# Fused attention and two feed-forward layers on one core: last block's bias rows doubled by DMA, first weight units split on ScalarE and VectorE, four small items moved within a step

## The chip, the cores and the metric

The kernel runs on one core of a Trainium2 chip. The metric is the device time of one execution in microseconds (us). The time before is the median of three executions. The profile is of one more execution of the same program.

## The reference

Attention with a learned relative-position bias, then two feed-forward layers, all in float32. B = 2, H = 8, S = 576, D = 64; 1152 tokens, model width 512, hidden width 2048.

```python
scores = (q @ k^T) / sqrt(D)                            # B, H, S, S
x = log1p(abs(i - j)) / log1p(max(i, 1))                # S, S
bias = relu(x * w1 + b1) @ w2                           # 32 hidden, then H
attn = softmax(scores + bias)
x = (attn @ v) as 1152 tokens x 512
h = x @ w_in;  x = (relu(h) + alpha * min(h, 0)) @ w_out
h = x @ w_in2; x = (P(h) / (Q(h) + 1e-6)) @ w_out2      # P cubic, Q quadratic in abs(h)
```

## The kernel before

**Blocks and steps.** The query rows are cut into nine blocks: four groups of 128 rows for each of the two batches, and a last block 8 that holds the remaining 64 rows of both batches. A block takes four steps, one for each pair of heads, so there are 36 steps, n = 0 to 35. In step n TensorE computes the scores of that step (L326) into PSUM, VectorE adds the bias and takes the row maximum (`row_max`, L338, once for each head of the pair: u = 0 and 1), ScalarE takes the exponential and its row sums (`expo`, L349), TensorE transposes the result (`flip` u = 0, 1 and 2, L365 and L361), ScalarE or VectorE copies the transposes out of PSUM (`flip_out`, L377 on ScalarE, L371 and L375 on VectorE), and TensorE multiplies with the values (L389). The steps overlap: the transposes of step n run in step n + 1 and its values in step n + 2. The scores have two PSUM buffers, one for each u; so the scores of step n + 1 wait for both row maxima of step n, and for `flip_out` 2, which reads a spare corner of the second buffer. After step 35 the same banks hold the first hidden tiles of the feed-forward part.

**Bias rows.** Beside the steps the bias of the next group of rows is made, one eighth in each step: `hidden` (L228 on ScalarE, L230 on VectorE), a matmul in two halves (`bias_mm`, L244, into a PSUM tile with a single buffer, so each half waits until the one before it has been copied out), the copies `bias_out` (L256 on ScalarE, L258 on VectorE) and a DMA that brings the rows into place (`bias_move`, L270). The last block has four such parts; two DMAs of 64 rows for each (L274) fill partitions 0 to 63 of the bias tile, for one batch, and `bias_again` (L278) copies them to partitions 64 to 127, two heads at a time, on VectorE, in steps 29 to 32.

**End of a block.** `inverse` (L400 to L402) inverts the row sums. For blocks 0 to 5 the inverse goes through a transpose (`inverse_flip`, L407) and DRAM to all partitions; from block 6 on `inverse_on_tensor` (L434) spreads it with 16 matmuls. `block_out` (L423) copies the values' result out of PSUM, `block_scale` (L442) multiplies it with the inverse on VectorE, and `block_split` cuts it into a high part (L450, ScalarE) and a low part (L451, GpSimd).

**Weights.** The weights come in units of 128 x 512, 64 in all. For each, `unit_load` (L603 or L605) loads it as pairs of words, `unit_rest` and `unit_scale` (L617, L613) work on ScalarE, `unit_join` (L621, L624) on VectorE; then `unit_high` rounds to the high part and `unit_low` subtracts it. For units 0 to 11 the high part is made on VectorE (L646) and the low part on GpSimd (L651); for the others on ScalarE (L644) and VectorE (L651). Units 0 to 4 are made during steps 30 to 35.

**Feed-forward part.** `up` (L682) and `down` (L697) matmuls run in pairs from step 35 on, each product as three matmuls of high and low parts.

**What sets the order.** The order of the instructions on each engine is written out by hand: each item gets a due time in an agenda, `ag.at(time, function, ...)`, and all items are issued in the order of these times. The times come from a table `Z` and from `step_time(n)`; they are no waits. Each engine runs its own instructions in this order and waits only for data and for buffers. So a change of a due time changes the place of an instruction in its engine's queue, and nothing else.

Of the kernel before, what the change touches and what calls it, by code (L numbers as in the profile page):

```python
# [11 lines left out]
F32 = mybir.dt.float32  # L12
# [4 lines left out]
ALU = mybir.AluOpType  # L17
# [3 lines left out]
B, H, S, D = 2, 8, 576, 64  # L21
# [29 lines left out]
def row_tables():  # L51
# [35 lines left out]
    
}
# [17 lines left out]
def fused_kernel(ctx: ExitStack, tc: tile.TileContext, qT, q4T, kT, vp, m1_in, m1_out, m2_in, m2_out, small, ttab, out):  # L106
    nc = tc.nc
# [9 lines left out]
    ag = Agenda()  # L117
# [96 lines left out]
    bias, hid, bev, bps = {}, {}, {}, {}  # L214
# [52 lines left out]
    def bias_move(j, r):  # L267
        be, bt = bev.pop((j, r)), bias[j]
        if j < 4:
            nc.sync.dma_start(out=bt[r::8].rearrange("p h j -> p (h j)"), in_=be)  # L270
        else:
            for i in range(2):
                rows = bt[2 * r + i : 64 : 8].rearrange("p h j -> p (h j)")
                nc.sync.dma_start(out=rows, in_=be[64 * i : 64 * i + 64])  # L274

    def bias_again(h):

        nc.vector.tensor_copy(out=bias[4][64:, h : h + 2], in_=bias[4][:64, h : h + 2])  # L278

    def bias_rows_beside(j, r, at, step, at0, step0):  # L280

        z, z0 = step / 4.1, step0 / 4.1
        for c in range(4):
            ag.at(at0 + z0 * Z[f"hidden{c}"], hidden, j, r, c)
        for u in range(2):
            x = at + Z[f"bias_mm{u}"] * z
            n = max((n for n in range(FIRST, LAST) if step_time(n) <= x), default=None)
            if n is None:
                ag.at(x, bias_mm, j, r, u)
                t = at + Z[f"bias_out{u}"] * z  # L290
            else:
                t = max(x, step_time(n) + Z["beside"])
                ag.at(t, bias_mm, j, r, u)
                key = "scalar" if f"bias_scalar_{j}{u}" in ON else "vector"
                t = max(step_time(n) + Z[f"bo_{key}{int(t - step_time(n) >= Z['values'])}"], t + 0.1)
            ag.at(t, bias_out, j, r, u)
        ag.at(max(at + Z["bias_move"] * z, t + 0.1), bias_move, j, r)

    def bias_rows(j, r, at, step, at0, step0):
        z, z0 = step / 4.1, step0 / 4.1  # L300
        for c in range(4):
            ag.at(at0 + z0 * Z[f"hidden{c}"], hidden, j, r, c)
        ag.at(at + Z["bias_mm0"] * z, bias_mm, j, r, 0)
        ag.at(at + Z["bias_out0"] * z, bias_out, j, r, 0)
        ag.at(at + Z["bias_mm1"] * z, bias_mm, j, r, 1)
        ag.at(at + (1.6 * step if j == 0 else Z["bias_out1"] * z), bias_out, j, r, 1)
        ag.at(at + Z["bias_move"] * z, bias_move, j, r)


    FIRST, LAST = 8, 36  # L310
# [115 lines left out]
    def by_tensor(k):  # L426
        return k >= 6
# [25 lines left out]
    DT, DT2, DT3 = 4.1, Z["dt2"], Z["dt3"]  # L453
# [16 lines left out]
    def step_time(n):  # L470
        t = T0
        for a, b, dt in ((0, 4, DT0), (4, 24, DT), (24, 32, DT2), (32, 99, DT3)):
            t += max(0, min(n, b) - a) * dt
        return t

    rows = [(0, r, Z["row0"] + r * Z["row_step"], Z["row_step"]) for r in range(8)]
# [11 lines left out]
    for n in range(NSTEP):  # L488
        t = step_time(n)
        k, hp = divmod(n, 4)  # L490
        next_t, new = step_time(n + 1), FIRST <= n + 1 < LAST
        ag.at(t, scores, n)
        for u in range(2):
            ag.at(t + Z["max0"] + Z["max1"] * u, row_max, n, u)
            ag.at(t + Z["expo0"] + Z["expo1"] * u, expo, n, u)
            ag.at(next_t + Z[f"new_flip{u}"] if new else t + DT + Z["flip0"] + Z["flip1"] * u, flip, n, u)
            ag.at(t + DT + Z["fout0"] + Z["fout1"] * u, flip_out, n, u)
        ag.at(next_t + Z["new_flip2"] if new else t + DT + Z["flip2"], flip, n, 2)
        ag.at(next_t + Z["new_fout2"] if new else t + DT + Z["fout2"], flip_out, n, 2)
        ag.at(t + 2 * DT + Z["values"], values, n)  # L500
        if hp == 3:
            ag.at(t + Z["inv"], inverse, k)
            scale = t + 3 * DT + Z["new_bscale"] if FIRST <= n + 2 < LAST else t + 3 * DT + Z["bscale"]
            if by_tensor(k):
                ag.at(scale - 0.1, inverse_on_tensor, k)
            else:
                at = step_time(n + 2) - 0.06 if FIRST <= n + 2 else t + DT + Z["iflip"]
                ag.at(at, inverse_flip, k)
                ag.at(at + 1.2, inverse_spread, k)
            ag.at(t + 3 * DT + Z["bout"], block_out, k)  # L510
            ag.at(scale, block_scale, k)
            ag.at(scale + Z["bsplit"] - Z["bscale"], block_split, k)
        if hp == 0 and k + 1 < len(BLOCKS):
            ag.at(t + Z["loadq"], load_q, k + 1)
# [5 lines left out]
    TAIL, TB = 3, Z["tb"]  # L520
    GB, NB, NT2 = 3, 3, 2
    NWA, NWC, NWB, NMID, NSP = 5, 2, 13, 13, 3
    UHS, USP = 12, 48
    NW = NWA + NWC + NWB
    t35 = step_time(NSTEP - 1)
    M0 = t35 + Z["m0"]
# [13 lines left out]
    now, p, d = M1, TAIL, 0  # L540
# [22 lines left out]
    wt, raws, mids, away = {}, {}, {}, {}  # L563
# [74 lines left out]
    def unit_high(j):  # L638
        slot = j % NW
        pool = pools["wa" if slot < NWA else "wc" if slot < NWA + NWC else "wb"][1]  # L640
        wt[units[j]] = pool.tile([P, 2, 512], F32R, tag="w", name="w")
        out = wt[units[j]][:, 0, :]
        if j >= UHS:
            nc.scalar.copy(out=out, in_=mids[j])  # L644
        else:
            nc.vector.tensor_copy(out=out, in_=mids[j])  # L646

    def unit_low(j):
        w = wt[units[j]]
        eng = nc.gpsimd if j < UHS else nc.vector  # L650
        eng.tensor_tensor(out=w[:, 1, :], in0=mids.pop(j), in1=w[:, 0, :].bitcast(F32), op=ALU.subtract)  # L651

    def early(j, key):
        return Z[key + "_early" * (j < NWA)]
# [7 lines left out]
    def unit_two(j, t):  # L662
        ag.at(t, unit_high, j)
        ag.at(t + early(j, "ulow"), unit_low, j)
# [126 lines left out]
        nc.vector.memset(one, 1.0 + 1e-6)  # L791

    ag.at(step_time(20), moe_consts)
    for h in range(0, H, 2):
        ag.at(step_time(29 + h // 2) + Z["again"], bias_again, h)
    ag.at(EARLY, early_pools)
    ag.at(M0 - 0.1, psum_u)
    ag.at(M1 - 0.1, late_psum)
# [9 lines left out]
    for p in range(NPAIR):  # L808
        ly, g, c, f = blocks[2 * p]
        t = u_t[2 * p + 1]  # L810
# [20 lines left out]
    for k in range(NU):  # L831
        ly, g, c, f = blocks[k]
        if f == groups[ly][g][-1]:
            for m in range(4 - ly):
                t = max(0.01 + 0.01 * m, HB * (m + 1) / (4 - ly) + Z[f"dadd{ly}"]) + d_t[k]
# [8 lines left out]
    for j in range(len(units)):  # L844
        t = one_t[-1] + Z["ud0" if j < 16 else "ud" if j < 22 else "ud2x"] if j else EARLY + Z["u0"]
        if j < NWA:
            t = max(t, two_t[j - 2] + early(j, "ulow") + 0.1 if j > 1 else 0.0)
        else:
            t = max(t, NEXT + 0.1 if j < NWA + NMID else two_t[j - NMID] + Z["ulow"] + 0.1 if j < USP else 0.0)
        one_t.append(t)  # L850
        t += early(j, "utwo")
        if j:
            t = max(t, two_t[-1] + early(j, "ud2"))
        if j >= NWA:
            t = max(t, NEXT + 0.1 if j < NWA + NWC else LATE + 0.2 if j < NW else released[j - NW] + 0.1)
# [67 lines left out]
```

## Time and profile before

| | |
|---|---|
| median of 3 executions | 604.25 us (603.94 to 604.37) |
| the profiled execution | 604.18 us |
| its span, first to last instruction | 602.4 us |
| around the span | 1.8 us |
| mean granted TensorE clock | 0.997 |
| busy: TensorE matmul / weight load | 586.9 / 504.3 us |
| busy: VectorE / ScalarE / GpSimd | 500.1 / 427.4 / 41.7 us |

In the profile PE is TensorE, PEld its weight load, DVE VectorE, ACT ScalarE, POOL GpSimd, and SP the engine that issues DMAs. Busy shares are averages over stages with different limits. Matmuls are pipelined, so a TensorE that shows as busy may still be waiting within a group; the distance from the scores of one step to those of the next shows more than the busy share does.

### The profile page before, as it was taken

To read this page: it belongs to the slowest core of one execution; us is meant where nothing else is said; L and a number is where in the kernel's file an instruction comes from. 1 tells how busy PE (TensorE), PEld (TensorE's weight loads), DVE (VectorE), ACT (ScalarE), POOL (GpSimd) and SP (SyncE) were. 2 spreads that over 40 slices of the span, in tenths; PEclk is the share of its full clock that TensorE was granted. 3 is DMA by queue.
4 is the path that set the end of the run, shared out by engine and by line. 5 is a ranking of instruction groups with operands and counts; after the bars stand their busy time and mean duration, and the time that the engine had idled before them with its cause. 6 is when DMAs were issued, how large, how long until landed. Compare 5 with 4: busy or idle time off the path is not lost.

```text
span 602.4 us, 11747 instructions
## 1 busy us (share of the span) xinstructions
PE 586.9 (97%) x4678; PEld 504.3 (84%) x4678; DVE 500.1 (83%) x837; ACT 427.4 (71%) x716; POOL 41.7 (7%) x35
## 2 busy tenths in 40 slices
PE   8899999999989999999999999999999999999997
PEld 5356666666767999999999999998999999899985
DVE  6687788887698967779998779989999999779783
ACT  6678889888777656576675567797777887655660
POOL 0000000000022321000000302100000000000000
PEclk9899999999999999999999999999999999999999
DMA  5893323342723334344555477767000000001011
GB/s 169 263 231 107 92 73 103 81 104 62 187 72 100 112 106 139 114 154 156 172 149 174 131 207 217 215 203 262 19 2 1 0 1 0 2 2 52 1 52 54
DMA packets 41239, 65.31 MB, mean 108 GB/s; under 512 B 4016, under 2 KB 23776, under 8 KB 41184
## 3 DMA queue, kind: packets, MB, share of 16 engines
q1 hardware_dynamic: 41040, 64.21, 36.4%
q8 instruction: 37, 0.61, 0.4%
q10 hardware_dynamic: 144, 0.35, 0.2%
q14 instruction: 18, 0.15, 0.1%
HBM read 47.35 MB, written 6.58 MB: 90 GB/s over the span
## 4 chain that ended last, share of the span: by engine, by line
PE 83%; DVE 8%; ACT 4%; DMA 2%; issue 2%; SPq 0%; ACTq 0%; DVEq 0%
PE ops L697 30%; PE hps L682 30%; PE bps L244 6%; PE s L326 5%; PE pv L389 5%; PE tp L365 4%; DVE p L338 1%; DVE mid L621 1%; PE s L361 1%; ACT pt L377 1%; DVE mid L624 1%; DMA away<-mid 1%; DVE w L651 1%; ACT p L349 1%; DMA bias<-be 1%
## 5 line engine op out<-in xcount | busy, mean ns | idle before, releaser
L682 PE MATMUL hps<-xh,w 128*128 128x384 f32 x768 | 204.1, 336 | 0.0
L682 PEld LDWEIGHTS hps<-xh,w 128*128 128x128 f32 x768 | 139.6, 188 | 1.3 <-issue 0.2
L682 PE MATMUL hps<-xl,w 128*128 128x384 f32 x384 | 128.7, 335 | 0.0
L697 PE MATMUL ops<-g,w 128*128 128x384 f32 x576 | 104.5, 336 | 0.0
L697 PE MATMUL ops<-w,g 128*128 128x512 f32 x432 | 102.5, 392 | 1.2 <-DVE acc L769 1.2
L697 PEld LDWEIGHTS ops<-g,w 128*128 128x128 f32 x576 | 100.8, 188 | 0.0
L697 PEld LDWEIGHTS ops<-w,g 128*128 128x128 f32 x432 | 80.7, 188 | 17.6 <-issue 1.5
L349 ACT ACTIVATE p<-p,nm 128x576 f32<-128x576 f32 x72 | 55.7, 773 | 28.1 <-DVE nm L338 28.0
L682 PEld LDWEIGHTS hps<-xl,w 128*128 128x128 f32 x384 | 72.1, 188 | 0.9
L752 ACT CAST g<-n 128x768 fp32r<-128x768 f32 x48 | 40.1, 835 | 40.0 <-DVE n L716 28.3
L338 DVE CUSTOM_DVE_ANT_0 p<-s,bias 128x576 f32<-128x576 f32 x72 | 52.1, 753 | 14.1 <-PE s L326 8.9
L621 DVE SCALAR_TENSOR_TENSOR mid<-mid,raw 128x512 int32<-128x512 int32 x64 | 50.4, 787 | 12.5 <-ACT mid L613 12.4
L244 PE MATMUL bps<-h,w2s 128*32 128x288 f32 x576 | 51.4, 421 | 5.0 <-DVE be L258 2.5
L230 DVE TENSOR_SCALAR h<-tt,sc,nb 128x576 f32<-128x576 f32 x98 | 53.4, 582 | 0.0
L757 DVE TENSOR_TENSOR g<-n,g 128x768 fp32r<-128x768 f32 x48 | 46.5, 968 | 7.8 <-ACT g L752 7.8
L624 DVE SCALAR_TENSOR_TENSOR mid<-raw,mid 128x512 int32<-128x512 int32 x64 | 50.3, 786 | 2.2
L326 PE MATMUL s<-kt,q 64*128 64x288 f32 (+1 forms) x320 | 46.1, 433 | 1.4 <-DVE nm L338 0.8
L389 PE MATMUL pv<-pt,v 128*32 128x128 f32 (+2 forms) x1200 | 46.8, 267 | 0.0
L389 PEld LDWEIGHTS pv<-pt,v 128*32 128x32 f32 (+1 forms) x1200 | 40.4, 119 | 7.3 <-issue 2.7
L617 ACT ACTIVATE raw<-raw 128x512 int32<-128x512 uint32 x64 | 43.4, 678 | 2.7 <-DMA raw<-in_moe_w_in_dram 1.4
L613 ACT ACTIVATE mid<-raw 128x512 f32<-128x512 f32 x64 | 42.4, 662 | 0.0
L228 ACT ACTIVATE h<-tt,sm,sc 128x576 f32<-128x576 f32 x46 | 39.3, 863 | 3.0 <-DVE sc L172 2.5
(75 smaller groups left out, 734.4 us busy)
## 6 DMA issues: line engine op xcount, KB each, us to landing
raw<-in_moe_w_in_dram SPq DMA_DIRECT2D x32, 512.0 KB, 4.6
raw<-in_moe_w_out_dram SPq DMA_DIRECT2D x32, 512.0 KB, 3.7
bias<-be SPq DMA_DIRECT2D x32, 288.0 KB, 4.1
away<-mid SPq DMA_DIRECT2D x16, 256.0 KB, 4.9
mid<-away SPq DMA_DIRECT2D x16, 256.0 KB, 4.2
v<-in_vp_dram SPq DMA_DIRECT2D x10, 256.0 KB, 6.8
kt<-in_kT_dram SPq DMA_DIRECT2D x8, 288.0 KB, 5.7
out_dram<-acc SPq DMA_DIRECT2D x9, 256.0 KB, 2.1
```

The costliest lines, as they stand in the source:

```text
L230: nc.vector.tensor_scalar(out=h, in0=x, scalar1=sc[:, k : k + 1], scalar2=nb1, op0=ALU.mult, op1=ALU.max)
L244: nc.tensor.matmul(out=ps[32 * c : 32 * c + 32], lhsT=w2s, rhs=hid[j, r, c][:, u * HALF : (u + 1) * HALF], start=True, stop=True,)
L326: nc.tensor.matmul(out=pps[n, u][cols, w, :HALF], lhsT=queries[k][rows, hp, cols], rhs=KT[bb][rows, hp, w * HALF : (w + 1) * HALF], start= ...
L338: nc.vector.tensor_tensor_reduce(out=ptile[n][:, u, :].rearrange("p (w j) -> p w j", w=2), in0=pps.pop((n, u))[:, :, :HALF], in1=bias[j][: ...
L349: nc.scalar.activation(out=p, in_=p, func=AF.Exp, bias=nms.pop((n, u)), scale=-1.0, accum_out=sums[k][:, h : h + 1])
L389: nc.tensor.matmul(out=pv[64 * u + d : 64 * u + d + wide, hp, cols], lhsT=V[bb][:, j, 2 * hp + u, d : d + wide], rhs=pt[:, 4 * u + j if j ...
L617: nc.scalar.activation(out=low, in_=low.bitcast(U32), func=AF.Copy, scale=0.90625 * 2.0 ** -29, bias=0.24)
L621: nc.vector.scalar_tensor_tensor(out=m, in0=m, scalar=3, in1=raw[:, :, 0], op0=ALU.logical_shift_left, op1=ALU.bitwise_or)
L624: nc.vector.scalar_tensor_tensor(out=m, in0=raw[:, :, 1], scalar=-(2 ** 31), in1=m, op0=ALU.bitwise_and, op1=ALU.bitwise_or)
L682: nc.tensor.matmul(out=ps, lhsT=a, rhs=b, start=(i == 0), stop=(i == len(prs) - 1))
L697: nc.tensor.matmul(out=ops[ly, c, m], lhsT=a, rhs=b, start=(f == fs[0] and i == 0), stop=(f == fs[-1] and i == 2))
L757: nc.vector.tensor_tensor(out=gt[:, 1], in0=tmp.pop(p), in1=gt[:, 0].bitcast(F32), op=ALU.subtract)
```

## The change

1. `bias_move` for the last block issues four DMAs of 64 rows for each of the four parts instead of two: each half of `be` goes to partitions 0 to 63 and again to 64 to 127. `bias_again` and its four calls are gone.
2. For units 0 to 11 `unit_high` now runs on ScalarE and `unit_low` on VectorE, as for the other units.
3. `bo_scalar0` goes from 2.9 to 2.35: the `bias_out` on ScalarE is issued earlier in its step. In the queue this passes it ahead of another instruction at two places: ahead of a `hidden` in step 24, and ahead of a `block_split` in step 27.
4. `inverse` of blocks 1 to 7 moves from 4.03 to 5.65 after the start of the block's last step (`new_inv`): from ahead of the next step's `row_max` to behind it and behind `flip_out` 2.
5. `block_scale` of blocks 1 to 5 moves from 3.3 to 5.8 (`new_bscale`), and `block_split` with it: `block_scale` from the end of one step to behind the next step's row maxima, the high part of `block_split` from ahead of that step's two `expo` to behind them. Blocks 6 and 7 keep 3.3 (`new_iscale`).

The lines of the table `Z` that hold these numbers are left out of the diff.

```diff
         else:
-            for i in range(2):
-                rows = bt[2 * r + i : 64 : 8].rearrange("p h j -> p (h j)")
-                nc.sync.dma_start(out=rows, in_=be[64 * i : 64 * i + 64])
-
-    def bias_again(h):
-
-        nc.vector.tensor_copy(out=bias[4][64:, h : h + 2], in_=bias[4][:64, h : h + 2])
+            for o in (0, 64):
+                for i in range(2):
+                    rows = bt[o + 2 * r + i : o + 64 : 8].rearrange("p h j -> p (h j)")
+                    nc.sync.dma_start(out=rows, in_=be[64 * i : 64 * i + 64])
...
         if hp == 3:
-            ag.at(t + Z["inv"], inverse, k)
-            scale = t + 3 * DT + Z["new_bscale"] if FIRST <= n + 2 < LAST else t + 3 * DT + Z["bscale"]
+            ag.at(t + (Z["new_inv"] if FIRST <= n + 1 < LAST else Z["inv"]), inverse, k)
+            scale = t + 3 * DT + Z["bscale"]
+            if FIRST <= n + 2 < LAST:
+                scale = t + 3 * DT + Z["new_iscale" if by_tensor(k) else "new_bscale"]
...
         out = wt[units[j]][:, 0, :]
-        if j >= UHS:
-            nc.scalar.copy(out=out, in_=mids[j])
-        else:
-            nc.vector.tensor_copy(out=out, in_=mids[j])
+        nc.scalar.copy(out=out, in_=mids[j])
 
     def unit_low(j):
         w = wt[units[j]]
-        eng = nc.gpsimd if j < UHS else nc.vector
-        eng.tensor_tensor(out=w[:, 1, :], in0=mids.pop(j), in1=w[:, 0, :].bitcast(F32), op=ALU.subtract)
+        nc.vector.tensor_tensor(out=w[:, 1, :], in0=mids.pop(j), in1=w[:, 0, :].bitcast(F32), op=ALU.subtract)
...
-    for h in range(0, H, 2):
-        ag.at(step_time(29 + h // 2) + Z["again"], bias_again, h)
```

## Rows read from the trace of the kernel before

**Rows 1.** The page's chain that ended last, shares of the span by engine

```profile
PE 83%; DVE 8%; ACT 4%; DMA 2%; issue 2%; SPq 0%; ACTq 0%; DVEq 0%
```

**Rows 2.** Busy time by stretch: start:end, length, each engine's busy us (instructions), clock, DMA

```profile
170.00:180.00 10.00, 7.76 (x92) 5.29 (x90) 9.52 (x20) 6.31 (x14) 4.44 (x3) 1.00 0.24 80
180.00:190.00 10.00, 8.58 (x131) 6.35 (x129) 7.68 (x20) 7.59 (x17) 1.92 (x2) 1.00 0.32 107
190.00:200.00 10.00, 10.00 (x125) 9.41 (x125) 9.42 (x16) 6.92 (x13) 3.62 (x3) 1.00 0.26 69
```

**Rows 3.** Timeline, steps 11 to 13: start, length, instruction, [idle before, releaser]

```profile
76.32 1.24 PE L326 MATMUL s<-kt,q 64*128 64x288 f32 x8
...
80.87 1.24 PE L326 MATMUL s<-kt,q 64*128 64x288 f32 x8
...
81.64 0.20 DVE L401 RECIPROCAL rs<-rs 128x8 f32<-128x8 f32 x1
...
82.45 0.75 DVE L338 CUSTOM_DVE_ANT_0 p<-s,bias 128x576 f32<-128x576 f32 x1
...
85.92 1.24 PE L326 MATMUL s<-kt,q 64*128 64x288 f32 x8
```

**Rows 4.** Timeline, step 15 and the start of step 16

```profile
95.07 1.24 PE L326 MATMUL s<-kt,q 64*128 64x288 f32 x8
...
97.05 0.61 ACT L450 CAST xh<-xu 128x512 fp32r<-128x512 f32 x1
...
99.97 1.24 PE L326 MATMUL s<-kt,q 64*128 64x288 f32 x8
```

**Rows 5.** Timeline, the end of step 24

```profile
140.96 0.86 ACT L228 ACTIVATE h<-tt,sm,sc 128x576 f32<-128x576 f32 x1
...
142.27 0.69 PE L244 MATMUL bps<-h,w2s 128*32 128x288 f32 x8 [1.38 <-ACT be L256]
```

**Rows 6.** Timeline, steps 32 and 33

```profile
171.44 1.73 POOL L651 TENSOR_TENSOR w<-mid,w 128x512 fp32r<-128x512 f32 x1
171.51 0.69 PEld L326 LDWEIGHTS s<-kt,q 64*64 64x64 f32 x16 [0.17 <-issue]
...
172.07 1.65 DVE L624 SCALAR_TENSOR_TENSOR mid<-raw,mid 128x512 int32<-128x512 int32 x1
...
173.75 0.75 DVE L278 COPY bias<-bias 64x1152 f32<-64x1152 f32 x1
...
175.06 0.75 DVE L338 CUSTOM_DVE_ANT_0 p<-s,bias 128x576 f32<-128x576 f32 x1
...
179.22 0.33 PE L361 MATMUL s<-ident,p 128*128 128x128 f32 x1 [0.84 <-ACT p L349]
```

**Rows 7.** Timeline, the end of step 34 to the first feed-forward matmul

```profile
186.73 1.09 PE L434 MATMUL tp<-ident,rs 128*64 128x128 f32 x16 [0.29 <-ACT pt L377]
...
189.14 0.75 DVE L338 CUSTOM_DVE_ANT_0 p<-s,bias 128x576 f32<-128x576 f32 x1
189.36 1.28 POOL L451 TENSOR_TENSOR xl<-xu,xh 128x512 fp32r<-128x512 f32 x1 [6.18 <-ACT xh L450]
...
189.96 0.44 PE L682 MATMUL hps<-xh,w 128*128 128x384 f32 x1
```

**Rows 8.** Groups by form, the two weight parts: count, busy us, mean ns, idle before

```profile
L651 DVE TENSOR_TENSOR w<-mid,w 128x512 fp32r<-128x512 f32 x52 | 35.5, 684 | 0.0
L644 ACT CAST w<-mid 128x512 fp32r<-128x512 f32 x52 | 31.9, 616 | 10.8 <-PE hps L682 10.8
```

**Rows 9.** Tile views: issue of the bias DMAs (min/median/max ns); landing of weight loads

```profile
L274 SPq DMA_DIRECT2D bias<-be x8: 597/600/644, 142.2 to 156.8; - x8
...
DMA to landing us min/median/max: 3.6/3.7/4.8
```

**Rows 10.** Timeline: issue of the first weight load, and its first reader

```profile
157.49 0.41 SPq L603 DMA_DIRECT2D raw<-in_moe_w_in_dram  x1
...
163.95 0.66 ACT L617 ACTIVATE raw<-raw 128x512 int32<-128x512 uint32 x1
```

More of the change, by code (lines that the diff above doesn't have):

```diff
@@ L522, in fused_kernel @@
     NWA, NWC, NWB, NMID, NSP = 5, 2, 13, 13, 3
-    UHS, USP = 12, 48
+    USP = 48
     NW = NWA + NWC + NWB
```

2 rows, old and new, of the table Z are left out of this document.

## The prediction

> **What bounds the kernel now.** I read the chain of waits first. TensorE is 83% of it, VectorE 8%, ScalarE 4% [rows 1]: a change elsewhere is worth only what TensorE stops waiting for. Then the busy time by stretch: TensorE idles 2.24 us in 170 to 180 and 1.42 us in 180 to 190, and from 190 on it is full [rows 2]. So nearly all the idle time that the edits could reach lies in steps 32 to 35, where VectorE is busy 9.52 of 10 us. Last the timeline, since in the earlier steps TensorE shows as busy while it waits: there I measure from the scores of one step to the next. A regular step takes 76.32 to 80.87, 4.55 us [rows 3], which is the sum of its matmuls. What exceeds that, and what the edits take away of it, is the first part of the gain; steps 32 to 35 are the second.
>
> **The change part by part: steps 8 to 31.** Step 12 takes 80.87 to 85.92, 5.05 us [rows 3]. It holds an inverse flip of 0.20 (the end of a block), so 0.30 is excess. The scores end at 82.11, but the first row maximum starts at 82.45: the three instructions of the inverse (the one shown takes 0.20, the other two a little less, 0.54 together) stand before it. Moved behind both maxima they find VectorE idle, and nobody reads the inverse before the next step's flip. That returns 0.30. Against it, `block_split`'s ScalarE part of 0.61 [rows 4] (0.5 from start to start) now stands between the second exponential and the copy-out of the step before, and the second half of the transposes needs that copy's PSUM buffer; by the starts around step 12 the copy would end 0.1 late. Net 0.2. Steps 16 and 20 have the same pattern, with less and more excess. Together 0.5; bounds 0 (the copy eats it) and 0.9.
>
> Step 15 takes 95.07 to 99.97, 4.90 us [rows 4]: 0.35 over a regular step. `block_split` at 97.05 stands ahead of the exponential, which could have started half a microsecond earlier. Moved behind both exponentials it is off that path: 0.35, bounds 0 and 0.35. The scale itself goes to a place behind the maxima where VectorE has slack before the next bias copy.
>
> Step 24: TensorE waits 1.38 us for ScalarE's bias copy [rows 5]. The copy comes right behind a `hidden` of 0.86 (start to start 0.77), which the new `bo_scalar0` puts behind it: 0.77 back. The inverse leaves the path to the exponential: another 0.54 at most. But block 4's split now stands before this exponential as well, 0.5 later. The inverse's gain and the split's loss nearly cancel, and in the trace ScalarE has some slack there: I take 1.0; bounds 0.25 (0.77 less the split) and 1.3.
>
> Sum of this part: 0.5 + 0.35 + 1.0 = 1.85, bounds 0.25 and 2.55. Steps 28 to 31 stay as they are: TensorE runs them without idle time.
>
> **Steps 32 to 35.** The matmuls of the scores of step 32 begin at 171.51 and run about 1.2 us, but the first maximum starts at 175.06 [rows 6]. In between VectorE finishes a join: L624 starts at 172.07 and takes 1.65, while GpSimd's low part runs from 171.44 to 173.17; VectorE's instruction ends 0.55 after GpSimd's. A part of that size otherwise takes about 0.7 (L651's mean is 0.684 [rows 8]), so about 0.95 is waiting for GpSimd. Then `bias_again`, 0.75, and the inverse, 0.54. All three go, and so does the VectorE copy of unit 0 ahead of the maximum of step 31. That is 2.24 and more, so the maximum is bounded by the scores, at 172.7, and by the join behind GpSimd's part of block 6, which stays and starts some 0.4 later because ScalarE now makes unit 0's high part first. I take 172.95, a gain of 2.1.
>
> This gain goes down the chain. The wait for the exponential at 179.22 [rows 6] moves with it, as does a second one of the same kind a step on. ScalarE gets a high part in each of these steps, 0.616 [rows 8]: unit 0's costs 0.1 on the path, unit 1's falls into time in which ScalarE waits for the maximum, unit 2's stands before the second exponential of step 33 and takes 0.5, unit 3's falls behind the copy that releases the spreading matmuls. Of the 0.5 the spreading matmuls at 186.73 give back 0.29, their own wait [rows 7]: they and the scores of step 35 come 2.05 earlier. There VectorE has a new instruction: unit 2's low part (0.684, start to start 0.6) ahead of the first maximum of step 35. So that maximum comes 2.05 - 0.65 = 1.4 earlier than 189.14. The first feed-forward matmul at 189.96 [rows 7] takes the PSUM banks of that maximum and begins as it ends, so it comes 1.4 earlier too. Bounds: 0.2 (below) and 3.66, all the idle time of both stretches [rows 2].
>
> From there TensorE has no idle time [rows 2], and everything behind it shifts as a whole: VectorE loses the locked time of eleven more GpSimd parts, ScalarE has room. The low parts of units 3 to 11 come later than before but ahead of their matmuls, by the order of the agenda.
>
> Here the profile is weighed against a rule. VectorE's instruction above ended 0.55 after GpSimd's [rows 6]. In the Trainium skill, SBUF — State Buffer, section Who interferes with whom, a VectorE instruction with two SBUF inputs and a GpSimd one that reads SBUF exclude each other, and the second to start blocks. By that, the trace agrees, and the rule speaks against the new low parts on VectorE: beside GpSimd's part of a block they can be held for a whole instruction. In the sum above none is held.
>
> **The four DMAs.** Two more issues for each of the four parts, 0.600 each [rows 9]; the last part is copied out near 156, so its rows are in place long before step 32 reads them at 172.95. On SP the first weight load waits behind them: 157.49 becomes 1.2 later, lands at most 4.8 after its issue [rows 9, 10], at 163.5, and ScalarE reads it at 163.95: hidden, with 0.45 to spare. The block's query load behind it has until step 32.
>
> **Sum.** 1.85 + 1.4 = 3.25 us. The profiled execution took 604.18 (span 602.4 and 1.8 around it), so 600.9; the median of the runs is 604.25, 0.07 above it, so 601.0. The unknown costs give 0.45 to 6.2 us of gain, 603.8 to 598.1.
>
> **Rivals.**
>
> *More of the idle time goes* (599.4). Speaks for it: 3.66 us of idle time, and the exponentials only wait for maxima that come 2.1 earlier. Then the first part is 1.85, and the second 3.0. Against it: ScalarE's extra high part in each step.
>
> *A new wait takes the second part* (602.4). GpSimd's part of block 7 starts 2.63 after the spreading matmuls do (189.36 - 186.73), and the maximum, whose place the new low part takes, 2.41 after (189.14) [rows 7]: the low part is first by 0.22. If it comes second, it waits for GpSimd's 1.28, and the maximum with it: the second part falls from 1.4 to about 0.1. The same is left if ScalarE's high parts, 4 times 0.5, all fall on the path: 604.25 - 1.85 = 602.4. Against it: the order follows from one event, the end of the spreading matmuls, and ScalarE's part comes after VectorE's.
>
> *The first load comes late* (606.5, slower). If the extra DMAs held the queue for a landing each, 3.6 [rows 9] and not only for their issue, the load would land 7.2 later, 5.55 past its spare 1.65 (163.95 - 157.49 - 4.8). ScalarE's queue, with the exponentials of step 30 behind the load's reader, would stand for that time: 601.0 + 5.55 = 606.5. It makes the kernel slower by 0.2% from 6.1 us of delay on. Against it: the issues of the bias DMAs take 0.600 in the median and 0.644 at most [rows 9], so none stood for a landing. A rule points to it: the Trainium skill, DMA: Bandwidth & Descriptors, section Anatomy of one DMA, gives each DMA a fixed cost of about 2.0 us beside its bytes; two more of 144 KB in sequence would then be, as an estimate from that page, 4.7 us, 3.05 past the spare time, and 604.05, between this case and no change. No run here shows it yet.
>
> *Nothing moves* (604.25): the edits to steps 12 to 24 are eaten by the split's new place, and a smaller delay of the load takes the rest.
>
> **How the numbers follow.** The forecast 48% (own range 600.2 to 601.7), more 16%, new wait 20%, nothing 8%, late load 8%. The likeliest gives 601.0 us. Leaving out the late load, no change, and the far end of "more", the range that holds 8 in 10 is 599.2 to 603.0. About 0.2%, 1.2 us, is what a measurement can tell from no change: faster than 603.04 has 0.84, within it 0.09, slower 0.07 (the late load at its worst).
>
> **What the changed profile would show.** Right: steps 12 and 20 near 4.85 us and step 15 near 4.55; no hidden of ScalarE ahead of the bias copy in step 24, and TensorE's wait there 0.4 at most; L278 and GpSimd's L651 gone; L624 never above 1.0 beside step 32; the first maximum of step 32 within 0.4 of the end of its scores; the stretch from the scores of step 32 to the first feed-forward matmul 17.0 us rather than 18.45. Wrong: ScalarE idle before L617 for a DMA; the copy-outs holding the transposes by more than 0.2 in steps 12, 16, 20 and 24; a low part on VectorE over 1 us; TensorE waiting in 200 to 230 for a weight part made late.

## The result and the profile after

The changed kernel takes 612.26 us (median of four executions, 611.55 to 612.85) against 604.11 (four of the kernel before): a ratio of 1.0134, 95% interval 1.0117 to 1.0152. It is 1.3% slower, where 601.0 was forecast. The profiled execution took 612.85 us, its span 611.0. Line numbers move by a few: the scores are L324, the first reader of a loaded unit is L617 as before, the DMAs of the bias rows L276.

Where the time went is seen in one view. The timeline of the changed kernel, steps 28 to 32, with the last undisturbed matmuls ahead of the gap:

```profile
154.71 1.24 PE L324 MATMUL s<-kt,q 64*128 64x288 f32 x8
...
160.56 1.31 PE L387 MATMUL pv<-pt,v 128*64 128x128 f32 x20
...
161.80 1.24 PE L324 MATMUL s<-kt,q 64*128 64x288 f32 x8
...
171.23 0.65 ACT L617 ACTIVATE raw<-raw 128x512 int32<-128x512 uint32 x1 [8.74 <-DMA raw<-in_moe_w_in_dram]
...
172.33 0.57 ACT L421 COPY xu<-pv 128x512 f32<-128x512 f32 x1
...
172.96 2.40 PE L387 MATMUL pv<-pt,v 128*64 128x128 f32 x20 [8.78 <-ACT xu L421]
...
175.14 1.92 PE L432 MATMUL tp<-ident,rs 128*64 128x128 f32 x16
...
176.99 2.15 PE L324 MATMUL s<-kt,q 64*128 64x288 f32 x8
...
181.45 1.20 PE L324 MATMUL s<-kt,q 64*64 64x288 f32 x16
```

ScalarE waits 8.74 us for the first weight load. Before, the same instruction ran at 163.95 [rows 10] without a wait. `block_out`, queued behind it, comes at 172.33, and the values' matmuls wait for that: TensorE is idle for 8.78 us. A second loss follows. The values take 2.40 instead of 1.31, the spreading matmuls 1.92 instead of 1.09 [rows 7], the scores 2.15 instead of 1.24: together 2.83. The clock column of the next view says why.

SP's timeline of the changed kernel (issues of DMAs):

```profile
140.68 2.59 SPq L276 DMA_DIRECT2D bias<-be  x4
...
148.68 1.30 SPq L416 DMA_DIRECT2D rb<-rd  x2
150.07 9.32 SPq L276 DMA_DIRECT2D bias<-be  x12
159.49 0.41 SPq L603 DMA_DIRECT2D raw<-in_moe_w_in_dram  x1
```

Busy time of the changed kernel by stretches of 4 us, with 152 to 158 once more by itself; the last three columns are the granted clock, the busy share of the 16 DMA engines, and GB/s:

```profile
150.00:154.00 4.00, 4.00 (x61) 2.60 (x57) 2.45 (x7) 2.37 (x7) 0.00 (x0) 1.00 0.53 143
154.00:158.00 4.00, 4.00 (x65) 3.15 (x57) 2.19 (x8) 3.47 (x9) 1.28 (x1) 1.00 0.54 122
158.00:162.00 4.00, 4.00 (x45) 3.01 (x43) 2.46 (x8) 3.08 (x8) 0.00 (x0) 1.00 0.67 136
162.00:166.00 4.00, 2.17 (x17) 1.45 (x15) 1.65 (x5) 0.49 (x2) 0.00 (x0) 1.00 1.12 178
166.00:170.00 4.00, 0.00 (x0) 0.00 (x0) 0.00 (x0) 0.00 (x0) 0.00 (x0) 0.83 1.00 145
170.00:174.00 4.00, 1.04 (x10) 1.05 (x12) 1.39 (x2) 2.77 (x6) 0.00 (x0) 0.50 0.79 233
174.00:178.00 4.00, 4.00 (x34) 3.50 (x32) 0.69 (x1) 3.09 (x8) 0.00 (x0) 0.50 0.49 150
178.00:182.00 4.00, 4.00 (x46) 2.75 (x46) 2.79 (x7) 2.48 (x6) 1.27 (x1) 0.89 0.00 1
...
152.00:158.00 6.00, 6.00 (x92) 4.75 (x93) 4.12 (x13) 4.60 (x11) 1.28 (x1) 1.00 0.53 125
```

The issues are short: 12 take 9.32 us together, and the first load is issued at 159.49, 2.0 after [rows 10]. But from 150 to 158 the DMA engines stand at a share of 0.53 and 0.54, which is near what eight of sixteen engines give when they are full. The 143 GB/s of the first stretch hold two other DMAs too, the inverse's (L416, issued at 148.68); the rows alone move at 122 to 125 (154 to 158, 152 to 158). At that rate the 576 KB of one part (four DMAs of 144 KB) take 4.7 to 4.8 us, and the steps beside them take 4.60, 4.02 and 3.55 here. So the rows pile up.

How far they pile up can be counted. The view of the DMAs gives the pieces that moved, by size: first from the load's issue at 159.49 to 165, then from 165 to 171.23:

```profile
DMA packets 963, 0.93 MB, mean 168 GB/s; under 512 B 465, under 2 KB 721, under 8 KB 963
...
DMA packets 1296, 1.03 MB, mean 165 GB/s; under 512 B 571, under 2 KB 1178, under 8 KB 1296
```

The bias rows move in pieces of 2,304 bytes, the load in 512 pieces of 1 KB. After the load's issue 242 and 118 pieces of rows still move, 360 in all, or 5.6 of the DMAs of 144 KB. In the kernel before, the same view from 157.49 to 165 has 120. And until 165 exactly 256 pieces of the load's size move, which is half of the load. That fits a load of which one half runs on free engines at once and the other half waits for the engines that the rows fill.

From 166 to 170 the granted clock falls, after TensorE has been idle since about 164, and it stays at 0.50, the level of 1.2 GHz, from 170 to 178. That is where the slow matmuls stand.

Each part of the prediction outside the DMAs can still be read in this profile. Timeline of the changed kernel, steps 12, 16 and 24:

```profile
80.72 1.24 PE L324 MATMUL s<-kt,q 64*128 64x288 f32 x8
...
85.59 1.24 PE L324 MATMUL s<-kt,q 64*128 64x288 f32 x8
...
99.31 0.61 ACT L448 CAST xh<-xu 128x512 fp32r<-128x512 f32 x1
99.33 0.79 PEld L324 LDWEIGHTS s<-kt,q 64*128 64x128 f32 x8 [0.47 <-DVE h L230]
...
100.59 0.57 ACT L375 COPY pt<-tp 128x512 f32<-128x512 f32 x1
...
101.83 0.77 ACT L347 ACTIVATE p<-p,nm 128x576 f32<-128x576 f32 x1
...
104.44 0.54 PEld L324 LDWEIGHTS s<-kt,q 64*128 64x128 f32 x6
...
136.24 1.24 PE L324 MATMUL s<-kt,q 64*128 64x288 f32 x8
...
140.71 0.16 PEld L244 LDWEIGHTS bps<-h,w2s 128*32 128x32 f32 x8 [0.29 <-ACT be L256]
...
141.53 0.76 PE L324 MATMUL s<-kt,q 64*128 64x288 f32 x4
```

Step 12 takes 85.59 - 80.72 = 4.87 (5.05 before [rows 3]). Step 24 takes 5.29, where it took 6.30, and TensorE's wait for the bias copy is 0.29 instead of 1.38 [rows 5]. Step 16 is longer: 104.44 - 99.33 = 5.11, where it took 4.76. `block_split` at 99.31 and a `hidden` stand ahead of the copy-out at 100.59, and the first exponential starts 2.50 after the scores, where it started 2.13 after.

And the end of the attention part in the changed kernel:

```profile
195.58 1.20 PE L324 MATMUL s<-kt,q 64*64 64x288 f32 x16
...
197.57 0.75 DVE L336 CUSTOM_DVE_ANT_0 p<-s,bias 128x576 f32<-128x576 f32 x1
...
198.39 0.44 PE L678 MATMUL hps<-xh,w 128*128 128x384 f32 x1 [0.47 <-DVE nm L336]
```

From the scores of step 32 (181.45) to the first feed-forward matmul (198.39) it is 16.94 us. Before it was 18.45, forecast were 17.0.

### The profile page after: what moved, and what is told of

The parts are those of the page before. It is cut to its first block, busy times and chain, and to the rows that moved or that the text cites. A ratio compares the mean times of both kernels' runs of the same rounds, so it can differ in the third digit from the quotient of the medians.

```text
span 611.0 us, 11746 instructions
## 1 busy us (share of the span) xinstructions
PE 589.0 (96%) x4678; PEld 506.0 (83%) x4678; DVE 493.1 (81%) x833; ACT 433.6 (71%) x728; POOL 23.7 (4%) x23
## 4 chain that ended last, share of the span: by engine, by line
PE 83%; DVE 7%; DMA 4%; ACT 3%; issue 2%; SPq 0%; DVEq 0%; ACTq 0%
PE ops L693 30%; PE hps L678 29%; PE bps L244 6%; PE pv L387 6%; PE s L324 6%; PE tp L363 4%; DMA raw<-in_moe_w_in_dram 2%; DVE mid L621 1%; DVE p L336 1%; DVE w L647 1%; PE s L359 1%; DMA away<-mid 1%; ACT p L347 1%; ACT pt L375 1%; DMA bias<-be 1%
## 5 line engine op out<-in xcount | busy, mean ns | idle before, releaser
L621 DVE SCALAR_TENSOR_TENSOR mid<-mid,raw 128x512 int32<-128x512 int32 x64 | 47.1, 735 | 22.0 <-ACT mid L613 21.7
L617 ACT ACTIVATE raw<-raw 128x512 int32<-128x512 uint32 x64 | 43.4, 678 | 11.5 <-DMA raw<-in_moe_w_in_dram 10.1
L624 DVE SCALAR_TENSOR_TENSOR mid<-raw,mid 128x512 int32<-128x512 int32 x64 | 47.4, 741 | 2.2
L643 ACT CAST w<-mid 128x512 fp32r<-128x512 f32 x64 | 39.3, 616 | 10.7 <-PE hps L678 10.7
L324 PE MATMUL s<-kt,q 64*128 64x288 f32 (+1 forms) x320 | 46.4, 440 | 0.0
L647 DVE TENSOR_TENSOR w<-mid,w 128x512 fp32r<-128x512 f32 x64 | 44.6, 698 | 0.0
```

Of the source, the lines that this page charges most:

```text
L324: nc.tensor.matmul(out=pps[n, u][cols, w, :HALF], lhsT=queries[k][rows, hp, cols], rhs=KT[bb][rows, hp, w * HALF : (w + 1) * HALF], start= ...
L621: nc.vector.scalar_tensor_tensor(out=m, in0=m, scalar=3, in1=raw[:, :, 0], op0=ALU.logical_shift_left, op1=ALU.bitwise_or)
L624: nc.vector.scalar_tensor_tensor(out=m, in0=raw[:, :, 1], scalar=-(2 ** 31), in1=m, op0=ALU.bitwise_and, op1=ALU.bitwise_or)
L647: nc.vector.tensor_tensor(out=w[:, 1, :], in0=mids.pop(j), in1=w[:, 0, :].bitcast(F32), op=ALU.subtract)
```

## The experiments

Medians are compared with executions of the kernel before on the same chip (its medians: 604.05 for the first four experiments; 604.28 for the loads in another queue, the sixteen engines and the two parts of the second gain; 603.99 for unit 0 later and for the due times with sixteen engines; 603.96 for the last pair). In many executions, of the kernel before too, the granted clock dips once near the start of the program (0.83 from 20 to 30 us in the profile of before). Where it doesn't, as in the profile of the change without the doubled DMAs, everything behind comes up to 1.8 us earlier (the scores of step 2 begin at 29.94 there, at 31.74 in that of before), so steps are compared here by their distances.

**The doubled DMAs alone.** The kernel before with only the bias rows changed:

```diff
-            for i in range(2):
-                rows = bt[2 * r + i : 64 : 8].rearrange("p h j -> p (h j)")
-                nc.sync.dma_start(out=rows, in_=be[64 * i : 64 * i + 64])
+            for o in (0, 64):
+                for i in range(2):
+                    rows = bt[o + 2 * r + i : o + 64 : 8].rearrange("p h j -> p (h j)")
+                    nc.sync.dma_start(out=rows, in_=be[64 * i : 64 * i + 64])
...
-    for h in range(0, H, 2):
-        ag.at(step_time(29 + h // 2) + Z["again"], bias_again, h)
```

> The kernel before, with only the bias rows changed: four DMAs for each part, no copy on VectorE. Theory: ScalarE waits some 7 to 9 us for the first weight load, TensorE's clock falls while it idles, and without the other edits' gain the time is 612 to 615.5 us, at or above the changed kernel's. Rival (other edits cost the time): 603.3 us, since the copies on VectorE are gone.

Measured: 613.17 us, 1.0156 (1.0138 to 1.0173). ScalarE waits 7.34 us for the load. The loss is in this part of the change, and nothing else is needed for it.

**The change without the doubled DMAs.** The changed kernel with two DMAs for each part and `bias_again` on VectorE, as before:

```diff
-            for o in (0, 64):
-                for i in range(2):
-                    rows = bt[o + 2 * r + i : o + 64 : 8].rearrange("p h j -> p (h j)")
-                    nc.sync.dma_start(out=rows, in_=be[64 * i : 64 * i + 64])
+            for i in range(2):
+                rows = bt[2 * r + i : 64 : 8].rearrange("p h j -> p (h j)")
+                nc.sync.dma_start(out=rows, in_=be[64 * i : 64 * i + 64])
...
+    for h in range(0, H, 2):
+        ag.at(step_time(29 + h // 2) + Z["again"], bias_again, h)
```

> The changed kernel, with only the bias rows undone: two DMAs for each part and the copy on VectorE, as before. Theory (the doubled bias DMAs delay the first weight load, and nothing else costs time): the load lands before ScalarE needs it, no wait for a DMA on ScalarE. The 1.55 us that steps 8 to 28 gained in the changed kernel stay, and steps 32 to 35 gain 0.3 to 0.9, since the copies of 0.75 are back on VectorE: 601.9 us (601.3 to 602.6). Rival (the unit parts moved to ScalarE and VectorE, or the moved items, cost the time): 606 us or more.

Measured: 602.91, 0.9984 (0.9972 to 0.9996). The load is in time and the loss gone, but it is 1.0 above what was expected. (Of the 1.55 named in the expectation, the edits account for 1.3; the changed kernel's profile was 0.3 ahead already at step 8, 62.17 against 62.47.) From the scores of step 32 to the first feed-forward matmul it takes 18.78, more than the 18.45 of before: with the copies on VectorE the second part of the gain doesn't come.

**The second half by other DMAs.** As the last, but the second half is filled by four DMAs from 64 partitions to 64, two heads each, issued behind the second weight load:

```diff
-        nc.vector.tensor_copy(out=bias[4][64:, h : h + 2], in_=bias[4][:64, h : h + 2])
+        nc.sync.dma_start(out=bias[4][64:, h : h + 2], in_=bias[4][:64, h : h + 2])
...
-        ag.at(step_time(29 + h // 2) + Z["again"], bias_again, h)
+        ag.at(step_time(29) + 0.6 + 0.01 * h, bias_again, h)
```

> The changed kernel, but the second half of the bias tile is filled by four DMAs of 64 partitions to 64 partitions (two heads each), issued after the second weight load; two DMAs for each part as before. The same bytes move as in the changed kernel. Theory (the DMAs that write 8 partitions run at about half of the DMA engines' share, 0.53, and 16 of them outrun what that half drains, so the load stands behind them in the same rings): the first load lands as in the kernel before, no wait on ScalarE, 600.5 us (599.8 to 601.5). Rival (the bytes themselves are too many for the DMA engines in this stretch): a load is still late by 2 us or more, and the time is above 603.

Measured: 600.98, 0.9953 (0.9939 to 0.9967). The same bytes reach the same partitions by DMA, and the kernel is faster than both. So the bytes as such aren't the trouble; where their DMAs run, where they stand in the queue or when they move is.

**The due times alone.** The kernel before with `bo_scalar0`, `new_bscale`, `new_iscale` and `new_inv` as in the change (only the changed entries of `Z`; the lines that read them are those of the change):

```diff
...
-"bo_scalar0": 2.9
+"bo_scalar0": 2.35
-"new_bscale": 3.3
+"new_bscale": 5.8, "new_iscale": 3.3, "new_inv": 5.65
...
```

> The kernel before, with only the four due times changed (the bias copy on ScalarE, the inverse, the scaling and its split). Theory: steps 8 to 28 gain 1.55 us as in the changed kernel's trace (scores of step 28 at 154.7 and not 156.3), steps 32 to 35 gain 0.3 to 0.6 from the inverse alone: 602.3 us (601.9 to 602.8). Rival (the gain is given back at steps 32 to 35, where VectorE is full): 603.5 to 604.3.

Measured: 602.73, 0.9978 (0.9968 to 0.9987): 1.32 us by the medians.

**The loads in another queue.** The changed kernel, with

```diff
-            nc.sync.dma_start(out=raw.rearrange("p (k f) w -> p k (f w)", k=4), in_=src)
+            eng = nc.gpsimd if j < 3 else nc.sync
+            eng.dma_start(out=raw.rearrange("p (k f) w -> p k (f w)", k=4), in_=src)
```

> The changed kernel, all four DMAs for each part, but the first three weight loads are issued on GpSimd's DMA queue instead of SP's. Theory: the first load is late because its packets stand in SP's queue behind the packets of the bias DMAs, which drain at half of the 16 engines; in another queue they needn't wait for their turn, so the load lands 4 to 7 us after its issue, at 162 to 165, ScalarE waits for it 0 to 3 us rather than 8.7, and the time is 601 to 604. Rival: the engines themselves are full, whatever the queue: then ScalarE still waits some 8 us and the time stays at 611 to 613.

Measured: 610.04, 1.0087 (1.0071 to 1.0103). Its timeline, and then what its queue of GpSimd (q0) moved from 157.23 to 164 and from 164 to 168.59 (pieces, MB, share of 16 engines):

```profile
157.23 0.89 POOL L604 DMA_DIRECT2D raw<-in_moe_w_in_dram  x1
...
168.59 0.65 ACT L618 ACTIVATE raw<-raw 128x512 int32<-128x512 uint32 x1 [6.04 <-DMA raw<-in_moe_w_in_dram]
...
q0 software_dynamic: 72, 0.26, 24.0%
...
q0 software_dynamic: 72, 0.26, 19.4%
```

The theory as it stood falls. Issued 2.3 earlier and in a queue of its own, the load still lands some 11 us after its issue, and ScalarE waits 6.04. The place in SP's queue is a small part of the delay at most; the rival, that the engines themselves are full, is nearer. Here too one half of the load's 512 KB has moved by 164 and the other half comes after that.

**The same bytes on sixteen engines.** The rows of the last block are put in another order, so that the 16 rows of a part go to every fourth partition. Then one DMA of all 128 source partitions fills one half of the tile, to 16 partitions instead of 8; queries and output rows are arranged to match:

```diff
             for o in (0, 64):
-                for i in range(2):
-                    rows = bt[o + 2 * r + i : o + 64 : 8].rearrange("p h j -> p (h j)")
-                    nc.sync.dma_start(out=rows, in_=be[64 * i : 64 * i + 64])
+                rows = bt[o + r : o + 64 : 4].rearrange("p h j -> p (h j)")
+                nc.sync.dma_start(out=rows, in_=be)
...
-    given["q4T"] = q[..., 4 * P :]
+    given["q4T"] = q[..., [4 * P + 2 * (p % 4) + p // 32 + 32 * (p // 16 % 2) + 8 * (p // 4 % 4) for p in range(64)]]
...
```

> The changed kernel with the rows of the last block in another order of partitions (queries and output rows are arranged to match), so that each part goes to 16 partitions a batch with one DMA from all 128: two DMAs of 128 packets for each part rather than four of 64, the same bytes. Theory: a DMA to 8 partitions runs on 8 of the 16 engines only, and four of them take longer than a step; to 16 partitions it runs on all, the same bytes take half the time, no queue builds up, ScalarE doesn't wait for the first load by more than 1 us, and the time is 601.0 (600.0 to 602.0), as with the second half by wide DMAs. Rival: it is the bytes, or the writes to both halves of the bias tile, that keep the load back: 609 to 613. Second rival: it is the number of DMAs in SP's queue (this has two a part, as before): 601 too, which the time can't tell apart, but the share and rate of the DMA engines can: near 115 GB/s in the drain if it is the number, twice that if it is the engines.

Measured: 601.06, 0.9941 (0.9924 to 0.9957). Its busy time by stretch, to be laid beside that of the changed kernel:

```profile
150.00:154.00 4.00, 4.00 (x61) 2.50 (x53) 2.15 (x7) 2.37 (x7) 0.00 (x0) 1.00 0.99 255
154.00:158.00 4.00, 4.00 (x69) 3.15 (x63) 2.23 (x8) 3.47 (x10) 1.29 (x1) 1.00 0.50 129
```

and its timeline:

```profile
155.01 1.24 PE L323 MATMUL s<-kt,q 64*128 64x288 f32 x8
...
156.42 0.57 SPq L602 DMA_DIRECT2D raw<-in_moe_w_in_dram  x1
...
162.70 0.66 ACT L616 ACTIVATE raw<-raw 128x512 int32<-128x512 uint32 x1
...
170.25 1.20 PE L323 MATMUL s<-kt,q 64*64 64x288 f32 x16
...
171.59 0.75 DVE L335 CUSTOM_DVE_ANT_0 p<-s,bias 128x576 f32<-128x576 f32 x1
...
187.25 0.45 PE L677 MATMUL hps<-xh,w 128*128 128x384 f32 x1 [0.47 <-DVE nm L335]
```

From 150 to 154 the share is 0.99 at 255 GB/s, where four DMAs to half as many partitions gave 0.54 at 122 (154 to 158 there). ScalarE reads the first unit at 162.70 without a wait. That settles the second rival too: it isn't the number of DMAs, since the rate doubles at the same bytes, and the kernel before, with two DMAs for each part, stood at half the share as well (below). In the Trainium skill, DMA: Bandwidth & Descriptors, section Why a DMA increments its semaphore by 16 and not by 1, a DMA's engines are the largest number up to 16 that divides the slowest dimension of both its sides, on SP's queue always the lowest-numbered ones: by that, 8 partitions get 8 engines, always the same 8, and 16 get all. The shares of 0.54 and 0.99 agree; no row here names the single engines.

For comparison, the kernel before with its two DMAs for each part:

```profile
150.00:154.00 4.00, 4.00 (x70) 2.67 (x70) 2.28 (x6) 3.32 (x8) 0.60 (x1) 1.00 0.52 136
154.00:158.00 4.00, 4.00 (x67) 2.93 (x66) 2.17 (x9) 2.97 (x7) 0.68 (x1) 1.00 0.33 65
...
152.00:155.00 3.00, 3.00 (x33) 1.94 (x29) 2.50 (x7) 1.94 (x5) 1.28 (x1) 1.00 0.54 128
```

The half share was there before (0.54 from 152 to 155), but these engines came to rest between two parts (0.33 from 154 to 158), and the load met a third of the rows that it meets in the changed kernel (120 pieces against 360).

**Where the wait bites.** The changed kernel with ScalarE's and VectorE's work on unit 0 due 3.4 us later, its load where it was:

```diff
         ag.at(t - Z["uload"], unit_load, j)
+        t += 3.4 if j == 0 else 0.0
         ag.at(t, unit_scale, j)
```

> The changed kernel with one thing moved: ScalarE's and VectorE's work on unit 0 is due 3.4 us later (the load is issued at the same place). Theory: nobody needs unit 0 in step 31; the kernel stands only because the reader of the late load is ahead of the copies and exponentials of step 30 and 31 in ScalarE's queue. So ScalarE reaches the reader some 3.4 later, at 165.5 to 166, the load lands near 171 as in the changed kernel, ScalarE's wait falls from 8.7 to about 5.3, and the time from 612.3 to 608.9 (608.0 to 609.7); the granted clock still falls behind the wait. Rival: the late bias rows or queries hold the steps as well, behind ScalarE: then the time stays within 1 us of 612.3.

Measured: 608.11, 1.0069 (1.005 to 1.0088). ScalarE's timeline:

```profile
172.66 0.65 ACT L617 ACTIVATE raw<-raw 128x512 int32<-128x512 uint32 x1 [5.09 <-DMA raw<-in_moe_w_in_dram]
```

The wait falls from 8.74 to 5.09 and the time by 4.15 (612.26 and 608.11). The late unit wasn't missed by any matmul; the kernel stood only because the load's reader is in front of `block_out` and the exponentials in ScalarE's queue. The clock still falls (0.66 in 170 to 180).

**The parts of the second gain.** The units' move alone, on the kernel before:

```diff
-    UHS, USP = 12, 48
+    UHS, USP = 0, 48
```

> The kernel before with one part of the change alone: the high parts of units 0 to 11 on ScalarE and the low parts on VectorE; bias rows and due times as before. Theory now: VectorE, which is the busy engine of steps 29 to 34, wins the locked time of GpSimd's parts and loses as much by the low parts, so this is worth nothing alone: 604.1 (603.6 to 604.7). The prediction's rival: the move is worth about half of the second part by itself: 603.2 or less.

Measured: 604.10, 0.9999 (0.9989 to 1.0009): nothing. In its profile a loss and a gain cancel: from the scores of step 32 to the first feed-forward matmul it takes 18.78 instead of 18.45, and from there to the end 412.05 instead of 412.43. And the bias rows alone, the edit of the wide DMAs on the kernel before:

> The kernel before with two DMAs for each part, and bias_again as four DMAs of two heads each, 64 partitions to 64 partitions, issued behind the second weight load; nothing on VectorE for it, units and due times as before. Theory: VectorE's four copies of 0.75 are what steps 29 to 32 pay for; alone worth 1.9 (the difference of the two experiments of before that differ in it): 602.2 (601.5 to 602.9). Rival: without the units' move VectorE only falls from one wait for GpSimd into the next, so the last copy's 0.7 at most is won: 603.3 to 604.

Measured: 604.00, 0.9995 (0.9986 to 1.0004): nothing that is clear of the noise either, and the expected 1.9 falls. The timelines of VectorE show why. First with the wide DMAs alone, then with the units alone:

```profile
169.87 1.48 DVE L646 CAST w<-mid 128x512 fp32r<-128x512 f32 x1
171.27 0.74 DVE L338 CUSTOM_DVE_ANT_0 p<-s,bias 128x576 f32<-128x576 f32 x1
...
174.54 0.76 DVE L338 CUSTOM_DVE_ANT_0 p<-s,bias 128x576 f32<-128x576 f32 x1
```

```profile
170.70 1.40 DVE L621 SCALAR_TENSOR_TENSOR mid<-mid,raw 128x512 int32<-128x512 int32 x1
...
172.85 0.75 DVE L278 COPY bias<-bias 64x1152 f32<-64x1152 f32 x1
...
174.16 0.75 DVE L338 CUSTOM_DVE_ANT_0 p<-s,bias 128x576 f32<-128x576 f32 x1
```

With the copies gone, unit 0's high part, still on VectorE, takes 1.48 ahead of the second maximum of step 31, and the first maximum of step 32 comes 3.08 after its scores began (171.46), after 3.55 before [rows 6]. With the units gone, a `bias_again` and the inverse stand there, and it is 2.75 (scores at 171.41). With both and the due times it is 1.34 (171.59 - 170.25 in the kernel with sixteen engines). VectorE's queue in steps 31 to 32 is too long by more than either part; only together, and with the due times, do they bring the maximum back to the scores.

Then the due times and the sixteen-engine DMAs without the units' move, and both kernels again, side by side in more rounds:

> The kernel before with the four due times and with the bias rows of the last block by two DMAs of 16 partitions for each part (no bias_again), but units 0 to 11 split on VectorE and GpSimd as before. Theory: the bias rows are worth 1.8 only together with the units' move, since GpSimd's low parts still lock VectorE beside steps 31 to 34; so this is the moves, 1.3, and the 0.3 that the wide DMAs gave alone: 602.6 (602.0 to 603.2). Rival: the two gains add up without the units: 600.9 to 601.5, and the units' move is for nothing.

> The kernel with sixteen-partition DMAs (whole change otherwise) once more, on the same chip as the next one, in more rounds, since the two differ by 0.18% in runs on different chips, within their intervals. Theory: the units' move is worth something once the bias rows are off VectorE: this is 0.9941 (0.993 to 0.995) and the next 0.6 to 0.9 us above it. Rival: the units' move is worth nothing here either, both at 0.995 within 0.3 us of each other.

> The kernel before with the four due times and sixteen-partition DMAs, units on VectorE and GpSimd as before, on the same chip as the run ahead. Theory: 0.6 to 0.9 us above it, 0.9955 (0.9945 to 0.9965). Rival: within 0.3 us of it.

Measured: 601.71, 0.9959 (0.9943 to 0.9976), so the expected 602.6 falls: beside the due times, which take the inverse out of that queue, the bias rows are worth 1.0 without the units (602.73 less 601.71; the stretch from the scores of step 32 to the first feed-forward matmul falls from 18.34 to 17.32). In the pair, the kernel with the units' move takes 600.68, 0.9946 (0.9935 to 0.9958), that without 601.39, 0.9953 (0.9941 to 0.9965). The medians differ by 0.71 and 0.65 in the two comparisons and the spans by 0.7 and 0.8, but the intervals overlap: a gain of the units' move of some 0.7 is likely, not settled. The profiles of the pair put 0.3 of it before the first feed-forward matmul (17.00 against 17.30 from the scores of step 32) and 0.4 behind it (412.02 against 412.45 to the end). The changed kernel with sixteen-partition DMAs, 3.3 us under the kernel before, and that with the wide DMAs (0.9953) are the best versions found; their intervals overlap.

## Why the prediction was wrong

**The four DMAs: this step failed.** It priced two more DMAs for each part by their issue, 0.600 each, and bounded the landing of the load by 4.8 from loads that had found the engines free [rows 9]. The issues were sized nearly right (0.638 in the median, the load issued 2.0 later instead of 1.2). Not priced was how long the data takes on the engines: the engines that carry these rows were already full, at 0.54 of all, while a part was moving, with a pause behind each part, and doubling the bytes took the pause away. The load landed about 11.7 after its issue (159.49 to 171.23) instead of 4.8. The prediction's own first sign of being wrong, ScalarE idle before L617 for a DMA, is what the profile shows.

**What it cost.** TensorE's idle time of 8.78 and 2.83 by the lower clock make 11.6. From the scores of step 28 to the first feed-forward matmul the changed kernel takes 198.39 - 154.71 = 43.68, that with sixteen engines 187.25 - 155.01 = 32.24: 11.4 more. The forecast of 601.0 and these 11.4 make 612.4; 612.26 was measured. The step named a cover of 0.45 us; it didn't name what TensorE's clock would take beyond the cover.

**The rival "the first load comes late"** had the place (ScalarE's queue in front of the load's reader) and the sign, with a chance of 8%. Its mechanism didn't occur: no issue of these rows stood for a landing (0.889 at most). Its price of 5.55 was half of what a filled queue costs. The estimate worked out there from the Trainium skill's fixed cost of a DMA, 604.05, is not borne out by 612.26. That section fits the cost to DMAs issued from GpSimd, and these rows go through SP's queue; what delayed the load was a steady share of 0.53 at 125 GB/s from 152 to 158, the rate at which the rows' bytes move.

**Steps 8 to 31: right in kind, 1.3 instead of 1.85.** The due times alone gave 1.32. Step 12 gave 0.18 (0.2 forecast), step 15 0.30 (0.35), step 24 1.01 (1.0). Steps 16 and 20 cancel: step 20 gave 0.34, but step 16 lost 0.35, because the split's 0.5 on ScalarE delays copy-out and exponential there. The prediction saw that loss in step 12, at 0.1, and didn't work it out for step 16; the bound "0 (the copy eats it)" was the truth for that pair. Steps 8, 11 and 19, which the prediction left alone, lost 0.08, 0.05 and 0.05.

**Steps 32 to 35: right.** 1.4 was forecast at the first feed-forward matmul. The stretch from the scores of step 32 took 17.0 as forecast (16.94 in the changed kernel, 17.00 in those with wide or sixteen-partition DMAs), 1.45 less than before. The first maximum of step 32 started 0.14 after its scores ended (170.25 and 1.20, 171.59). "A new wait takes the second part" didn't come: no GpSimd part held the low part ahead of the maximum of step 35. Nor did "more of the idle time goes". The rule on VectorE and GpSimd that was weighed there shows once: the longest low part takes 1.61 (at 215.51, beside GpSimd's part of a block from 215.28 to 216.57, and again 0.55 past its end), far behind the steps, and the mean of all 64 stays at 0.698.

**The sum.** Of 3.25 forecast for all that isn't the DMAs, 3.28 came where the DMAs were repaired (603.96 - 600.68). That the two agree is luck in part. The parts are 1.3, where 1.85 was forecast, 1.45, and about 0.4 behind the first feed-forward matmul, which the prediction held to shift as a whole; two misses cancel. The 0.4 comes with the units' move: from the first feed-forward matmul to the end it takes 411.99 to 412.09 in the five kernels that have this move and no late load, and 412.43 to 412.59 in the six without the move, that of before among them. Which wait returned it isn't shown.

**Still open.** In the queue of GpSimd the load was late too, though not as much. In both queues one half of the load moved early and the other half late, which fits eight free engines and eight full ones, though no row names the engines. Why in the other queue the late half had no turn beside the rows before 164, and what share the order within SP's queue had in the 8.74, no run tells apart.

## What to carry to other kernels

A DMA costs not only its issue but the time on the engines that it runs on: before doubling transfers, look at the DMA share in that stretch. A steady 0.5 can be eight full engines, as it was here, and not half of the room. A landing time measured on free engines is no bound behind a queue; give a load's reader a place in its engine's queue where nothing urgent stands behind it. And when one engine's queue is too long by several items, the worth of each item must be worked out with the others still there: two edits worth nothing alone were worth 1.75 us together beside the due times (602.73 - 600.98), where the units' move by itself gave nothing (602.91) and the bias rows by themselves 1.0.

## What the runs showed of the hardware

DMAs of 144 KB to 8 partitions moved 122 to 125 GB/s at a share of 0.54 and 0.53 of the 16 engines, DMAs of 288 KB to 16 partitions 255 GB/s at 0.99, with the same source rows of 2,304 bytes (576 floats). While TensorE stood idle for 8.78 us the granted clock fell to 0.50, and it was still there from 174 to 178, though matmuls had been running again since 172.96: the wait cost 8.78 and the slower matmuls behind it another 2.83.
